# Fused linear attention and squared-ReLU MLP: the second product in f16 from chunk 3, f16 projections from pair 7, denominators summed on GpSimd, Strassen from chunk 13, two matmuls of constants first

## The chip, the cores and the metric

The kernel runs on one core of a Trainium2 chip. A core has five engines that run side by side: PE (TensorE, matrix products), DVE (VectorE), ACT (ScalarE), POOL (GpSimd) and SP (SyncE, which here issues all transfers between the device's memory and the core's own). Each works through its own list of instructions in order and waits on semaphores for the others. The metric is the device time of one execution in microseconds, as a median over runs; lower is better.

## The reference

Two stages. The attention has 8 batches and 8 heads of 576 tokens with 64 dimensions; the features are 128 projections, made positive by two exponentials. The MLP takes the 4608 tokens by 512 dimensions through 2048 hidden units.

```python
def phi(x):
    proj = np.einsum('bhsd,df->bhsf', x, w_phi)
    proj = proj - np.max(np.abs(proj), axis=-1, keepdims=True)
    return np.concatenate([np.exp(proj), np.exp(-proj)], axis=-1)
q_p, k_p = (phi(q), phi(k))
kv = np.einsum('bhsf,bhsd->bhfd', k_p, v)
z = np.sum(k_p, axis=2)
num = np.einsum('bhsf,bhfd->bhsd', q_p, kv)
den = np.einsum('bhsf,bhf->bhs', q_p, z)[..., None] + 1e-06
x = (num / den)            # as 4608 tokens x 512
h = x @ w_in
g = np.maximum(h, 0.0) ** 2
out = g @ w_out
```

All inputs and the output are float32.

## The kernel before

**Attention by pairs.** Two heads of a batch make a pair; there are 32. The first six (`early`, line 779) go a way of their own while the weights are prepared. From pair 6 on, `visit(i)` (973) puts into one stretch of PE the key projections of pair i+1 (`k_main`, `k_tail`), the product of keys and values of pair i (`kv_main`) and the numerators of pair i-1 (line 989). `late(p)` (1036) projects the queries into `pt` (one buffer), finds the largest magnitude of each column with a GpSimd reduction over partitions (1088), subtracts, takes two exponentials into `qe`, and for the denominators weighs them by the key sums into `pt` again (1100, 1102). A transpose and a sum on DVE (1106, 1107), two transfers through device memory, a short DVE tail (1117 to 1120) and further transfers give 1/den as rows in `rb`. `tokens` (934) multiplies by the numerators, scales, and writes x as an f16 pair (high part and remainder) into `ring`.

Before pair 12 (`HALF`) the projections are float32 products. From pair 12 on `narrow` (655) finds the size of k and q (ACT, then a small GpSimd reduction), and splits each into an f16 high part and remainder; the projection is then three f16 products.

**MLP by chunks.** A chunk is 256 tokens (18 of them), a block is 256 hidden units of it (8 a chunk, 144 in all); `moe(c, f)` at 1138 makes one block. The first product, `gemm1` (1164), is 24 f16 matmuls of 256 columns: high by high, high by low, low by high. ACT and DVE form g = relu(h)^2 as `gh` in f32r (float32 bits that PE reads in one pass) and the remainder `gl` in bf16. The second product, `gemm2` (1195), is 12 matmuls of 512 columns: four in f32r against `wh`, eight in bf16 against `wl` and a bf16 copy of w_out. From chunk 14 (`C0`) on, `split_block` (1408) does the second product by Strassen's scheme in f16 instead: seven products of 128 x 256 in three parts, 21 matmuls of 256 columns (1440), with sums and differences on DVE before and after. Of the last chunk the last two blocks (`ENDS`) keep the plain way. Strassen needs bounds: `split_norms` (1253) takes column norms of w_in and row maxima of w_out, `tail_scale` (1289) the norms of a chunk of x, and from them a power of two for the chunk, so that g fits f16.

**The order.** Every step is added to a `Plan` (83) with the engine, an assumed duration, what it comes after and a rank. A planner in the program runs through these with its own clock per engine and writes each engine's list in that order. The ranks of nearly all steps come from a table of characters (`RANKS`) that was fixed beforehand; some steps can go to either of two engines (`other`), and the planner chooses. On the chip nothing is reordered: an engine that waits holds up all behind it.

Of the kernel before, what the change touches and what calls it, by code (L numbers as in the profile page):

```python
# [26 lines left out]
F = 128  # L27
# [7 lines left out]
T = 256  # L35
NCH = NT // T
C0 = 14
ENDS = 2
HALF = 12
LASTB = C0 * T // S  # L40
LOOK = (B - 1 - LASTB) * NP
RING = 6 * T
# [7 lines left out]
LEAD = 44  # L50
# [8 lines left out]
COLD = 1.1  # L59
# [23 lines left out]
class Plan:  # L83
# [73 lines left out]
    def order(self):  # L157
# [13 lines left out]
        mode, moved = WHOLE, 0.0  # L171
# [22 lines left out]
        while done < len(self.ops):  # L194
# [28 lines left out]
            op.start, op.end = t, t + us * (COLD if e == "PE" and t < 125.0 else 1.0)  # L223
# [61 lines left out]
def dve_us(n):  # L285
    return (n + 151) / 960

# [5 lines left out]
def par_us(n):  # L293
    return 0.45 + n * 0.0030
# [7 lines left out]
def tile_kernel(ctx, tc, qp, kp, vp, w_phi, w_in, w_out, out):  # L302
# [100 lines left out]

    pool_start = P.add("POOL", 10.8, lambda: None, [], [], -100.0)
# [166 lines left out]
    def batch_scale(b, rank):  # L571
# [63 lines left out]
    def narrow_weights(rank):  # L635
# [4 lines left out]
            wk[1], wk[0], channels=128, reduce_op=bass_isa.ReduceOp.max), [o, pool_next], [], rank, lock=0.0)  # L640
# [14 lines left out]
    def narrow(p, rank):  # L655
# [10 lines left out]
        o = P.add("POOL", par_us(2), bound, last + [pool_next], uses[:2], rank + 0.1, lock=0.0)  # L666
# [9 lines left out]
        for i, (tag, (raw, ld)) in enumerate(raws.items()):  # L676
# [257 lines left out]
    def tokens(p, nums, rank):  # L934
# [11 lines left out]
        for c0, c1 in cuts:  # L946
# [11 lines left out]
            def low(to=to, c0=c0, c1=c1):  # L958
# [4 lines left out]
                "DVE", dve_us(c1 - c0), lambda to=to, c0=c0, c1=c1: V.tensor_scalar(  # L963
# [72 lines left out]
    def late(p):  # L1036
# [48 lines left out]
        for h in range(2):  # L1085
# [4 lines left out]
                [pt[0], pt[1 + h], pool_next], [("pt", p), ("mx", n)], R(RQ + 0.2), lock=0.0)  # L1090
# [10 lines left out]
                out=y(), in_=qe(0), func=AF.Copy, scale=zc_[p][:, 2 * h:2 * h + 1]), [zc, o], use, R(RQ + 0.8))  # L1101
            o = P.add("DVE", dve_us(S), lambda h=h, qe=qe, y=y: V.scalar_tensor_tensor(  # L1102
# [3 lines left out]
            o = P.add("DVE", dve_us(S), lambda n=n, y=y: V.transpose(yt_["y", n - 2 * EARLY], y()), [o], [("pt", p), ("yt", ("y", n - 2 * EARLY))], R(RQ + 0.9))  # L1106
            dens.append(P.add("DVE", dve_us(S), lambda n=n, h=h: V.tensor_reduce(
                out=d4_[p][:, h, :], in_=yt_["y", n - 2 * EARLY].rearrange("p (b x) -> p b x", x=32), op=ALU.add, axis=AX.X),
                [o], [("yt", ("y", n - 2 * EARLY)), ("d4", p)], R(RQ + 1.0)))

        o = P.add("SP", 0.4, lambda: SP.dma_start(dd_[p], flat(d4_[p])), dens, [("d4", p), ("dd", p)], R(RQ + 1.1),
                  land=1.9, xfer=0.1)
        o = P.add("SP", 0.4, lambda: SP.dma_start(da_[p], dd_[p].rearrange("(a x) y -> x a y", a=4)), [o],
                  [("dd", p), ("da", p)], R(RQ + 1.1), land=1.9, xfer=0.1)

        def inverse():
            V.tensor_reduce(out=dr_[p][:, 0:36], in_=da_[p].rearrange("p a x -> p x a"), op=ALU.add, axis=AX.X)
            V.tensor_scalar(out=dr_[p][:, 0:36], in0=dr_[p][:, 0:36], scalar1=1e-6, scalar2=None, op0=ALU.add)
            V.reciprocal(out=dq[:, :, 0:18], in_=dr_[p].rearrange("p (h x) -> p h x", h=2))
            V.transpose(dt_[p], flat(dq))  # L1120

        use = [("da", p), ("dr", p), ("dt", p)]
        o = P.add("DVE", 0.95, inverse, [o], use, R(RQ + 1.1), lock=4.0)

        def keep():
            for h in range(2):
                SP.dma_start(rd_[p].rearrange("(h x) y -> h (x y)", h=2)[h].rearrange("(b x) -> b x", x=32),
                             dt_[p][0:18, 32 * h:32 * h + 32])

        o = P.add("SP", 0.7, keep, [o], [("dt", p), ("rd", p)], R(RQ + 1.1), land=1.9, xfer=0.1)  # L1130
        spread(p, o, lambda h: rd_[p].rearrange("(h c r) x -> h c (r x)", c=2, h=2)[h].unsqueeze(0).to_broadcast([64, 2, SH]),
               R(RQ + 1.1))


# [3 lines left out]
    def moe(c, f, w_done):  # L1138
# [15 lines left out]
        if f == 0 and split:  # L1154
            tail_scale(c, after)
# [497 lines left out]
```

## Time and profile before

| | us |
|---|---|
| median of 3 runs | 1032.64 (1032.29 to 1034.31) |
| the profiled execution | 1029.46 |
| its span, first to last instruction | 1027.7 |
| busy PE / DVE / ACT / POOL | 994.9 / 824.1 / 740.5 / 169.1 |

The profile is of one execution on its one core. Its page and the answers of its trace are read as follows. A line of the windows has the stretch, then the busy time of each engine in it. A line of the groups has the program line, engine, operation, written and read tiles, shapes, count, busy time and the mean ns of one, then the idle time of the engine ahead of it and what ended it. A line of the timeline or of the chain of waits has the start in us, the duration, and the instructions merged in it. Matmuls are pipelined: one lasts longer from start to end than the distance to the next start, so the cost of one is read from starts.

### The profile page before, as it was taken

How to read it: one execution, taken by the hardware profiler on the slowest of the kernel's cores; microseconds unless marked ns; L12 is line 12 of the kernel's file. 1: busy time of each engine (PE TensorE's matmuls, PEld its weight loads, DVE VectorE, ACT ScalarE, POOL GpSimd, SP SyncE). 2: the span in 40 equal slices, each digit the busy share in tenths (PEclk: the TensorE clock that was granted, in tenths of full speed). 3: DMA queues.
4: the chain of work that ended last, by engine and by line, in shares of the span. 5: the costliest groups of instructions: out<-in, count | busy, mean ns of one | idle time of the engine just before them, and what ended most of it. 6: DMA issues, size and time to landing. Idle time of an engine off the chain costs nothing. (4 is left out here: it accounts for less than half of the span.)

```text
span 1027.7 us, 21125 instructions
## 1 busy us (share of the span) xinstructions
PE 994.9 (97%) x8247; PEld 717.0 (70%) x8310; DVE 824.1 (80%) x1547; ACT 740.5 (72%) x1346; POOL 169.1 (16%) x100
## 2 busy tenths in 40 slices
PE   7879899999999999999999999999999999999998
PEld 5546666676766667667766667667667667888886
DVE  7999887867778885987989889798877889974463
ACT  7999876667678857768877878977667677664462
POOL 0122131031211102202111034311021110000000
PEclk9999999999999999999999999999999999999999
DMA  9744323222222321232323412222111110000000
GB/s 359 262 163 131 135 60 88 66 72 57 63 71 66 82 75 38 62 77 54 105 61 93 97 48 60 69 63 73 41 46 46 25 40 33 1 22 1 22 22 21
DMA packets 92936, 76.28 MB, mean 74 GB/s; under 512 B 61476, under 2 KB 70308, under 8 KB 90788
## 3 DMA queue, kind: packets, MB, share of 16 engines
q1 hardware_dynamic: 92836, 74.93, 25.1%
q8 instruction: 65, 1.06, 0.4%
q14 instruction: 35, 0.29, 0.1%
HBM read 61.18 MB, written 13.68 MB: 73 GB/s over the span
## 5 line engine op out<-in xcount | busy, mean ns | idle before, releaser
L1164 PE MATMUL ph<-ring,win 128*128 128x256 f16 x3456 | 391.8, 273 | 1.4 <-DVE gl L315 1.4
L1164 PEld LDWEIGHTS <-win 128*128 128x128 f16 x3456 | 336.0, 98 | 58.5 <-issue 9.8
L1088 POOL PARTITION_ALL_REDUCE mx<-pt x52 | 116.0, 2232 | 497.7 <-ACT pt L320 196.9
L1195 PE MATMUL po<-wh,gh 128*128 128x512 f32 x456 | 146.0, 441 | 0.0
L1195 PE MATMUL po<-wl,gl 128*128 128x512 bf16 x455 | 118.2, 382 | 0.1
L1176 ACT ACTIVATE r<-ph,cw 128x512 f32<-128x512 f32 x114 | 77.6, 681 | 55.5 <-PE ph L1164 55.1
L1195 PE MATMUL po<-wl,gh 128*128 128x512 bf16 x394 | 107.0, 379 | 5.9 <-issue 3.5
L315 DVE TENSOR_TENSOR gl<-ph,gh 128x512 bf16<-128x512 f32 x114 | 77.3, 678 | 34.9 <-ACT ph L1180 31.3
L1195 PEld LDWEIGHTS po<-wh,gh 128*128 128x128 f32 x456 | 86.1, 189 | 26.2
L1195 PEld LDWEIGHTS <-gh 128*128 128x128 bf16 x456 | 42.0, 98 | 49.1 <-issue 8.2
L1195 PEld LDWEIGHTS <-gl 128*128 128x128 bf16 x456 | 35.3, 98 | 58.3 <-issue 26.7
L1178 ACT ACTIVATE gh<-r 128x512 fp32r<-128x512 f32 x114 | 71.1, 624 | 3.7 <-PE po L1195 1.5
L1180 ACT ACTIVATE ph<-r 128x512 f32<-128x512 f32 x114 | 67.0, 588 | 0.4
L768 PE MATMUL pv<-e,v 128*64 128x256 f32 x512 | 62.8, 389 | 3.2 <-ACT kz L322 2.0
L315 DVE TENSOR_TENSOR qe<-pt,mx 128x576 f32<-128x576 f32 x52 | 39.0, 751 | 20.2 <-POOL mx L1088 18.7
L315 DVE TENSOR_TENSOR v<-qe,gh 128x896 f16<-128x896 f32 x30 | 32.6, 1089 | 27.2 <-ACT gh L1428 27.0
L1093 ACT ACTIVATE qe<-qe 128x576 f32<-128x576 f32 x52 | 35.2, 677 | 20.1 <-DVE qe L315 19.8
L1102 DVE SCALAR_TENSOR_TENSOR pt<-qe,zc,pt 128x576 f32<-128x576 f32 x52 | 42.1, 809 | 9.5 <-ACT pt L1100 9.2
L768 PEld LDWEIGHTS pv<-e,v 128*64 128x64 f32 x512 | 35.0, 141 | 20.7 <-ACT kz L322 2.9
L1413 ACT ACTIVATE r<-ph,cwr 128x512 f32<-128x512 f32 x30 | 20.6, 686 | 34.2 <-PE ph L1164 34.0
L1440 PEld LDWEIGHTS <-gh 128*128 128x128 f16 x420 | 41.1, 98 | 4.8
L1249 POOL PARTITION_ALL_REDUCE n<-n x12 | 22.2, 1848 | 119.3 <-DVE n L1247 79.7
(362 smaller groups left out, 1851.8 us busy)
## 6 DMA issues: line engine op xcount, KB each, us to landing
v<-in_vp_dram SPq DMA_DIRECT2D x32, 320.0 KB
k<-in_kp_dram SPq DMA_DIRECT2D x32, 288.0 KB
q<-in_qp_dram SPq DMA_DIRECT2D x32, 288.0 KB
rb<-rd SPq DMA_DIRECT2D x64, 144.0 KB
out_dram<-o SPq DMA_DIRECT2D x28, 256.0 KB
td<-kvs SPq DMA_DIRECT2D x26, 128.0 KB
kz<-td SPq DMA_DIRECT2D x104, 32.0 KB
zq<-zd SPq DMA_DIRECT2D x104, 2.0 KB
```

The source lines that it names most:

```text
L315: eng.tensor_tensor(out=out_, in0=a, in1=b_, op=ALU.subtract)
L768: PE.matmul(out=to[64 * h:64 * h + 64, 0:256], lhsT=v_[p][:, t, h, :], rhs=e_[2 * p + h][:, t].rearrange("p s f -> p (s f)"), start=t == 0 ...
L1088: o = P.add("POOL", par_us(S), lambda n=n, h=h: G.partition_all_reduce(mx_[n], pt_[p][:, h, :], channels=128, reduce_op=bass_isa.ReduceOp. ...
L1093: o = P.add("ACT", act_us(S), lambda qe=qe: A.activation(out=qe(1), in_=qe(0), func=AF.Exp, scale=-1.0), [o], [("qe", n)], R(RQ + 0.4))
L1102: o = P.add("DVE", dve_us(S), lambda h=h, qe=qe, y=y: V.scalar_tensor_tensor(out=y(), in0=qe(1), scalar=zc_[p][:, 2 * h + 1:2 * h + 2], in ...
L1164: PE.matmul(out=ph[:, j, :], lhsT=win[w][:, t, 128 * ff:128 * ff + 128], rhs=ring[half][x][:, t, c0:c0 + T], start=k == 0, stop=k == 3 * K ...
L1176: o = P.add("ACT", act_us(512, 1), lambda: A.activation(out=r_[n], in_=ph_[bank], func=AF.Relu, scale=cw[:, f, 0:1]), [g1], [("ph", bank), ...
L1178: sq = P.add("ACT", act_us(512), lambda: A.activation(out=gh_[n], in_=r_[n], func=AF.Square), [o], [("r", n), ("gh", n)], Q)
L1180: o = P.add("ACT", 0.59, lambda: A.activation(out=ph_[bank], in_=r_[n], func=AF.Square), [o], [("ph", bank), ("r", n)], Q, other=("DVE", 0 ...
L1195: PE.matmul(out=po_[po[i][1]], lhsT=g[:, j, 128 * i:128 * i + 128], rhs=w[:, j, :], start=(f == (NFP - ENDS if last else 0) and (s, j) == ...
L1249: o = P.add("POOL", par_us(T), lambda: G.partition_all_reduce(n2_[i], n1_[i], channels=128, reduce_op=bass_isa.ReduceOp.add), [o, pool_nex ...
L1440: PE.matmul(out=to, lhsT=l()[:, a], rhs=r(slice(b_, b_ + 1))[:, 0], start=(f == 0 and k == 0 and place % 2 == 0), stop=(f == NFP - 1 - END ...
```

## The change

The table of ranks is replaced, and with it the order of all engines' lists. The planner's assumptions change too: the largest ones are that PE is slow after the start and after a pause (`COLD`, `WARM`, `GAP`, `AGAIN`), that DVE is faster at one form of operation (`pair_us`), and that a GpSimd reduction over partitions and a DVE operation no longer exclude one another (`lock=None`). `LEAD`, a shift of the MLP's ranks, goes from 44 to 52.

- Two float32 matmuls of a constant tile, 480 columns each, stand first on PE.
- `HALF` 12 to 7: pairs 7 to 11 are narrowed and projected in f16.
- Denominators: the DVE transpose and sum, the tail and the transfers between are replaced by a GpSimd sum over partitions, one transfer per head, and the add and reciprocal that the early pairs use.
- From chunk 3 (`CS`) on, `gh` and `gl` are f16 and `gemm2` is three f16 parts. `narrow_out` rescales w_out to an f16 pair in place, after chunk 2. `chunk_scale` takes the place of `tail_scale` for all these chunks, and the first Relu of a block comes after it. `split_norms` is due before chunk 3.
- `C0` 14 to 13: chunk 13 goes by Strassen; `split_out` reads the f16 pair.

```diff
-C0 = 14
+C0 = 13
-HALF = 12
+CS = 3
+HALF = 7
-LEAD = 44
+LEAD = 52
...
+    def warm():
+        for i in range(2):
+            PE.matmul(out=po_[0][:, 0:480], lhsT=ones[:, 0:1].to_broadcast([128, 128]),
+                      rhs=ones[:, 0:1].to_broadcast([128, 480]), start=True, stop=True)
+
+    P.add("PE", 2.3, warm, [], [("po", 0)], -100.0)
...
-            o = P.add("DVE", dve_us(S), lambda n=n, y=y: V.transpose(yt_["y", n - 2 * EARLY], y()), [o], [("pt", p), ("yt", ("y", n - 2 * EARLY))], R(RQ + 0.9))
-            dens.append(P.add("DVE", dve_us(S), lambda n=n, h=h: V.tensor_reduce(
-                out=d4_[p][:, h, :], in_=yt_["y", n - 2 * EARLY].rearrange("p (b x) -> p b x", x=32), op=ALU.add, axis=AX.X),
...
-        o = P.add("DVE", 0.95, inverse, [o], use, R(RQ + 1.1), lock=4.0)
...
+            key = [("yt", ("y", n))]
+            o = P.add("POOL", 3.56, lambda n=n, y=y: G.partition_all_reduce(
+                yt_["y", n], y(), channels=128, reduce_op=bass_isa.ReduceOp.add), [o], [("pt", p)] + key,
+                R(RQ + 0.9), lock=None)
+            dens.append(P.add("SP", 0.5, lambda n=n, h=h: SP.dma_start(
+                den_[p][64 * h:64 * h + 64], yt_["y", n][0:1].rearrange("j (r x) -> j r x", x=9)), [o],
+                [("den", p)] + key, R(RQ + 1.0), land=2.1, xfer=0.1))
+
+        denominators(p, dens, lambda h: rd_[p].rearrange("(h c r) x -> h c (r x)", c=2, h=2)[h].unsqueeze(0).to_broadcast(
+            [64, 2, SH]), R(RQ + 1.1))
...
+        if f == 0 and c == CS:
+            for x in range(NFP):
+                narrow_out(x)
+        if f == 0 and c >= CS:
+            chunk_scale(c, after)
...
+        word = c >= CS
+        by = lambda: cw_[c][:, f:f + 1] if word else cw[:, f, 0:1]
+        gh = lambda: gh_.at(n, [128, 2, T], F16) if word else gh_[n]
+        gl = lambda: gl_.at(gi, [128, 2, T], F16) if word else gl_[gi]
+        use, wait = ([("cwr", c)], [norm_x[c]]) if word else ([], [])
...
+            if word:
+                lo, hi = wout[f][1].bitcast(F16), wout[f][2].bitcast(F16)
+                parts = (gh(), hi), (gh(), lo), (gl(), hi)
+            else:
+                low, near = wout[f][1:]
+                parts = (gh(), highs[f]), (upper(gh()), low), (gl(), near)
...
+        for i in range(2):
+            sums.append(P.add("ACT", act_us(512) + 0.19, lambda i=i: A.activation(
+                out=sx_["nx", 2 * c + i].bitcast(BF16)[:, 0:512].rearrange("p (k t) -> p k t", k=KT),
+                in_=ring[half][0][:, :, c0 + 128 * i:c0 + 128 * i + 128], func=AF.Square, accum_out=nx_[c][:, i:i + 1]),
+                after, [("sx", ("nx", 2 * c + i)), ("nx", c)], rank))
+        o = P.add("POOL", par_us(2), lambda: G.partition_all_reduce(
+            nx_[c][:, 4:6], nx_[c][:, 0:2], channels=128, reduce_op=bass_isa.ReduceOp.add), sums + [pool_next], [("nx", c)], rank, lock=None)
...
+    def narrow_out(f):
+        rank = LEAD + CS * NFP - 4.0 + f
+        places = lambda: (highs[f].bitcast(F32), wout[f][1], wout[f][2].bitcast(F16), wout[f][1].bitcast(F16))
...
+        def hi():
+            A.activation(out=places()[2], in_=places()[0], func=AF.Copy, scale=wts[:, 3:4])
+
+        def rest_of():
+            V.scalar_tensor_tensor(out=d(), in0=places()[0], scalar=wts[:, 3:4], in1=places()[2], op0=ALU.mult, op1=ALU.subtract)
+
+        def lo():
+            V.scalar_tensor_tensor(out=places()[3], in0=places()[1], scalar=wts[:, 3:4], in1=d(), op0=ALU.mult, op1=ALU.add)
+
+        o = P.add("ACT", act_us(1024, 1), hi, [g2_of[(CS - 1) * NFP + f], split_at["w"]], [], rank)
+        o = P.add("DVE", dve_us(1024), rest_of, [o], use, rank, lock=4.0)
+        narrow_w[f] = P.add("DVE", dve_us(1024), lo, [o], use, rank, lock=4.0)
...
-    split_norms(PER_PAIR * 24.0 + 3.0)
+    split_norms(LEAD + (CS - 2) * NFP)
```

More of the change, by code (lines that the diff above doesn't have):

```diff
@@ L58 @@
 RA, RQ, RZ = 1.3, 0.4, 0.3
-COLD = 1.1
+COLD = 1.8
+WARM = 5.0
+GAP = 2.6
+AGAIN = 5.5
 def word(x):
@@ L222, in order @@
             us, _, lock = op.ways[e]
-            op.start, op.end = t, t + us * (COLD if e == "PE" and t < 125.0 else 1.0)
+            if e == "PE" and t > max(cold, free["PE"] + GAP):
+                cold = t + AGAIN
+            op.start, op.end = t, t + us * (COLD if e == "PE" and t < cold else 1.0)
             if lock is not None:
@@ L664, in bound @@
             G.partition_all_reduce(x[:, 0:2], ka_[p], channels=128, reduce_op=bass_isa.ReduceOp.max)
-        o = P.add("POOL", par_us(2), bound, last + [pool_next], uses[:2], rank + 0.1, lock=0.0)
+        o = P.add("POOL", par_us(2), bound, last + [pool_next], uses[:2], rank + 0.1, lock=None)
         def bits():
@@ L1100, in late @@
             o = P.add("ACT", act_us(S, 1), lambda h=h, qe=qe, y=y: A.activation(
-                out=y(), in_=qe(0), func=AF.Copy, scale=zc_[p][:, 2 * h:2 * h + 1]), [zc, o], use, R(RQ + 0.8))
-            o = P.add("DVE", dve_us(S), lambda h=h, qe=qe, y=y: V.scalar_tensor_tensor(
+                out=y(), in_=qe(0), func=AF.Copy, scale=zc_[p][:, 2 * h:2 * h + 1]), [zc, o], use, R(RQ + 0.8), other=(
+                    "DVE", pair_us(S), lambda h=h, qe=qe, y=y: V.tensor_scalar(
+                        out=y(), in0=qe(0), scalar1=zc_[p][:, 2 * h:2 * h + 1], scalar2=None, op0=ALU.mult), 4.0))
@@ L1111, in late @@
[L1111 to L1120, printed above, removed]
@@ L1175, in moe @@
             return
+        word = c >= CS
[3 more added lines that the diff above has]
+        use, wait = ([("cwr", c)], [norm_x[c]]) if word else ([], [])
         o = P.add("ACT", act_us(512, 1), lambda: A.activation(
-            out=r_[n], in_=ph_[bank], func=AF.Relu, scale=cw[:, f, 0:1]), [g1], [("ph", bank), ("r", n)], Q)
-        sq = P.add("ACT", act_us(512), lambda: A.activation(out=gh_[n], in_=r_[n], func=AF.Square),
+            out=r_[n], in_=ph_[bank], func=AF.Relu, scale=by()), [g1] + wait, [("ph", bank), ("r", n)] + use, Q)
+        sq = P.add("ACT", act_us(512), lambda: A.activation(out=gh(), in_=r_[n], func=AF.Square),
                    [o], [("r", n), ("gh", n)], Q)
@@ L1211, in scaled @@
         def scaled():
+            if c >= CS:
+                V.tensor_scalar(out=o_[tt], in0=po_[po[1]], scalar1=ks_[c][:, i:i + 1], scalar2=None, op0=ALU.mult)
+                return
             k = cc[:, tt:tt + 1]
@@ L1215, in store @@
         if c < NCH - 1:
[L1216 removed]
+            o = P.add("DVE", dve_us(DM) + 0.11, scaled, [g2], [po, ("o", tt)] + ([("ks", c)] if c >= CS else []), Q)
             P.add("SP", 0.38, lambda: SP.dma_start(out[128 * tt:128 * tt + 128, :], o_[tt]), [o], [("o", tt)], Q,
@@ L1231, in tile_kernel @@
     wn = sm.tile([128, NFP], F32, name="wn")
-    cc2 = sm.tile([128, 1], F32, name="cc2")
-    last_cc = cc[:, 2 * NCH - 1:2 * NCH]
-    square_of = P.add("DVE", 0.2, lambda: V.tensor_tensor(out=cc2, in0=last_cc, in1=last_cc, op=ALU.mult), [], [], 250.0, lock=4.0)
     wnm = sm.tile([128, 2], F32, name="wnm")
@@ L1349, in split_out @@
             o = P.add("ACT", out_us(256 * n) + 0.09, lambda x=x, src=src: A.activation(
-                out=hi(x), in_=src(), func=AF.Copy, scale=wts[:, 3:4]), [o, split_at["w"]], key + us_ + keep, rank + 0.2)
+                out=hi(x), in_=src(), func=AF.Copy), [o], key + us_ + keep, rank + 0.2)
             o.after += home
-            o = P.add("DVE", dve_us(256 * n), lambda x=x, src=src: V.scalar_tensor_tensor(
-                out=lo(x), in0=src(), scalar=wts[:, 3:4], in1=hi(x), op0=ALU.mult, op1=ALU.subtract),
+            o = P.add("DVE", dve_us(256 * n), lambda x=x, src=src: sub(V, lo(x), src(), hi(x)),
                 [o], key + us_ + keep, rank + 0.3, lock=4.0)
@@ L1374, in sw_home @@
             return cut(*of[:4]), cut(*of[4:]), keep, []
-        g = f // 2
-        home = f"{'lh'[f % 2]}{g}"
-        wait = [("after", x) for x in (2 * g, 2 * g + 1)]
+        home = ("h0", "h1", "h2", "x1", "l0", "l1")[f]
+        wait = [("after", x) for x in (2 * f - 8, 2 * f - 7)] if f > 3 else []
         box = []
```

212 lines of the change are left out of this document (101 added, 111 removed).

## The prediction

> **What bounds the kernel now.** I read the windows first, by stage, because a share over the whole span mixes a start that waits for data with a long stretch that does not.
>
> ```profile
> 0.00:125.00 125.00, 103.19 (x1068) 71.43 (x1071) 108.27 (x173) 108.61 (x189) 17.55 (x12) 0.97 0.58 208
> 125.00:300.00 175.00, 173.18 (x1292) 118.80 (x1305) 140.54 (x277) 119.57 (x226) 32.91 (x17) 1.00 0.27 71
> 300.00:875.00 575.00, 569.80 (x4556) 395.57 (x4601) 486.12 (x924) 433.77 (x798) 115.01 (x69) 1.00 0.24 62
> 875.00:1028.00 153.00, 148.76 (x1338) 131.18 (x1336) 89.19 (x176) 78.50 (x137) 3.59 (x2) 1.00 0.04 15
> ```
>
> The columns are the stretch, its length, then the busy time of PE, PE's weight loads, DVE, ACT and POOL, the granted clock, the DMA share and GB/s. From 125 to 875 us PE is busy 743.0 of 750, so PE's own work sets the end there, and DVE and ACT have room. From 875 on PE is idle 4.2 us, nearly all of it the last result's way out. Before 125 us PE is idle 21.8 us: there the weights and the first pairs are prepared, and DVE and ACT (108 us each) share the bound with the loads. So an edit is worth what it takes out of PE's stream, plus what it changes in the 21.8 us at the start, plus any new stall: PE runs a list fixed in advance and waits in order.
>
> **PE's work.** The chain of waits and the PE timeline give the slots, from one start to the next.
>
> ```profile
> 684.97 2.67 PE po L1195 x12
> ...
> 892.04 1.31 PE pp L1440 x12
> 894.33 1.31 PE pp L1440 x12
> ...
> 923.15 13.10 PE ph L1164 x120
> ```
>
> ```profile
> 1020.08 1.04 PE L1195 MATMUL po<-wl,gl 128*128 128x512 bf16 x4
> 1020.96 0.59 PE L1195 MATMUL po<-wl,gh 128*128 128x512 bf16 x2
> ```
>
> ```profile
> 1020.74 0.38 PE L1195 MATMUL po<-wl,gl 128*128 128x512 bf16 x1
> ```
>
> A second product of one block is 12 matmuls of 512 columns in 2.67 us: 8 in bf16, 4 in f32r. The pace of 16-bit matmuls has three readings. The first product's f16 ones of 256 columns go at 13.10/120 = 0.109 us, hence 0.218 for 512. Four bf16 from 1020.08 to the next start at 1020.96 are 0.22 each. Two take 0.59 where one takes 0.38 from start to end, a step of 0.21. I take 0.216, among the three: twelve f16 make 2.59, so the f32r form costs 0.08 a block over it. The count: chunks 3 to 12 have 80 blocks, with the last chunk's two whole blocks 82, so **6.5 us** go. The ends are 0.03 a block (at 0.22: 2.5 us) and 0.15 (at 0.21: 12 us). This is the largest term and still small, since f32r already runs at nearly this pace; what goes is a few hundredths on 4 matmuls in 12.
>
> Chunk 13 changes to Strassen: 21 matmuls of 256 columns, whose blocks stand 894.33 - 892.04 = 2.29 apart, for 12 in 2.67. Eight blocks by 0.38 are **3.0 us**.
>
> ```profile
> 132.79 0.76 PE L1069 MATMUL pp<-q,wraw 64*128 64x288 f32 x4
> ...
> 133.96 1.04 PE L1195 MATMUL po<-wl,gh 128*128 128x512 bf16 x3
> ...
> 143.22 1.16 PE L703 MATMUL pp<-wraw,k 64*128 64x128 f32 x16
> 144.31 0.44 PE L715 MATMUL pn<-wraw,k 128*64 128x128 f32 x4
> 144.58 1.90 PE L768 MATMUL pv<-e,v 128*64 128x256 f32 x16
> ```
>
> ```profile
> 321.07 0.30 PE L1065 MATMUL pp<-q,whigh 64*128 64x288 f16 x2
> ...
> 321.91 0.50 PE L1164 MATMUL ph<-ring,win 128*128 128x256 f16 x3
> ```
>
> ```profile
> 687.57 0.23 PE L698 MATMUL pp<-whigh,k 64*128 64x128 f16 x2
> ...
> 688.53 1.68 PE L768 MATMUL pv<-e,v 128*64 128x256 f32 x14
> ```
>
> Pairs 7 to 11 go from f32 to f16 projections: q from 1.17 (132.79 to 133.96) to 0.84 (321.07 to 321.91), k from 1.36 (143.22 to 144.58) to 0.96 (687.57 to 688.53). Five pairs by 0.73 are **3.6 us**. Together PE loses 13.1 us.
>
> **The start.** Two matmuls of constants run while PE waits for the first k.
>
> ```profile
> 4.35 2.08 PE L703 MATMUL po<-wraw,k 64*128 64x128 f32 x16 [4.35 <-DMA k<-in_kp_dram]
> ...
> 11.79 2.95 PE L768 MATMUL pv<-e,v 128*64 128x256 f32 x16
> ...
> 22.76 1.95 PE L768 MATMUL pv<-e,v 128*64 128x256 f32 x16 [2.02 <-ACT kz L322]
> ...
> 32.52 1.16 PE L703 MATMUL po<-wraw,k 64*128 64x128 f32 x16
> ```
>
> The same groups take 2.08 at 4.35 us and 1.16 later, 2.95 at 11.79 and 1.95 later, so PE is about half as fast for its first 10 us. If the constants, inside the 4.35 us of waiting, end that, the groups to 15 us lose some 4 us. But 2 us of PE waiting for ACT at 22.76 follow, so part of it only lengthens waits. Between 0 and 4 I take 1.5, the start being bound by loads and by ACT and DVE as much as by PE.
>
> **DVE, ACT and POOL.** The groups by line:
>
> ```profile
> L1106 DVE STREAM_TRANSPOSE yt<-pt 128x576 f32<-128x576 f32 x52 | 40.0, 770 | 0.4
> ...
> L1107 DVE TENSOR_REDUCE d<-yt 128x18 f32<-128x576 f32 x52 | 38.5, 741 | 0.4
> ...
> L1247 DVE TENSOR_REDUCE n<-j 128x256 f32<-128x1024 bf16 x12 | 23.3, 1943 | 2.0 <-POOL n L1249 2.0
> ...
> L1249 POOL PARTITION_ALL_REDUCE n<-n x12 | 22.2, 1848 | 119.3 <-DVE n L1247 79.7 <-DVE xs L1296 24.0 <-DVE wn L1260 15.6
> ...
> L659 ACT ACTIVATE sx<-k 128x576 bf16<-128x576 f32 x20 | 13.6, 678 | 6.4 <-DMA k<-in_kp_dram 6.3
> ...
> L1117 DVE TENSOR_REDUCE dr<-da 32x36 f32<-32x144 f32 x26 | 10.0, 386 | 9.3 <-DMA da<-dd 9.3
> ...
> L1324 DVE TENSOR_TENSOR e<-wh,wl 128x1024 f32<-128x1024 f32 x8 | 9.5, 1210 | 0.0
> ...
> L664 POOL PARTITION_ALL_REDUCE kb<-ka x20 | 8.5, 425 | 18.1 <-ACT sx L659 15.5 <-DVE gl L315 2.5
> L670 DVE TENSOR_SCALAR kb<-kb 128x2 f32<-128x2 f32 x20 | 8.5, 423 | 5.8 <-POOL kb L664 5.6
> L1271 ACT ACTIVATE j<-wh 128x1024 bf16<-128x1024 f32 x8 | 8.4, 1050 | 1.8 <-DVE n L1247 1.8
> ```
>
> The denominators take off DVE 52 transposes and 52 sums, 78.5 us, and 26 short tails that begin with L1117 (10.0 us); the add and the reciprocal that replace the tails are of its kind. SP issues five transfers a pair for six. GpSimd gets 52 sums of 576 columns, which no run here has; its sums took 1.85 us for 256 columns, its small reduction 0.43 for 2, so by a straight line 0.43 + 574 x 0.0056 = 3.6 us, 189 us in all over some 700. GpSimd has the time (169 us busy now). For PE all this is worth nothing directly: DVE already had room.
>
> What comes in early is the load I weigh more. The norms of w_in and the row sums of w_out move from the middle to before chunk 3: 16 ACT passes of 1.05, 8 DVE sums of 1.94. The new rescaling of w_out costs 8 more ACT passes and 16 DVE passes of 1.21. Pairs 7 to 11 need two ACT sizes and two ACT roundings, about 0.75 each (an estimate from L659), and two DVE differences like it. That is 25 + 15 = 40 us of ACT and 16 + 19 + 8 = 43 of DVE, less some 20 of denominators, mostly into 125 to 300 us, where ACT and DVE have 260 of 350 busy: after it 323, 92%. I cost it at nothing, as PE has only 1.8 us idle there and chunks 0 to 2 stand ready as work; without that cover it is the second rival. The scale per chunk adds a wait ahead of each chunk's first Relu: two ACT passes, a short GpSimd reduction and a DVE chain; behind that Relu stand ACT's queue and then the second product. The ring's columns are written blocks ahead, and the first product (2.6 us) runs beside, so nothing again; if all 15 chunks waited 0.5 us, 7 us.
>
> **GpSimd against DVE.** Two rows of the timelines:
>
> ```profile
> 515.31 1.26 DVE L670 TENSOR_SCALAR kb<-kb 128x2 f32<-128x2 f32 x1 [0.73 <-POOL kb L664]
> ```
>
> ```profile
> 515.17 2.21 POOL L1088 PARTITION_ALL_REDUCE mx<-pt  x1
> ```
>
> A DVE instruction on two columns takes 1.26 us because a GpSimd reduction began 0.14 before it; it is let go at 516.57, 0.8 us before that reduction ends. So a reduction holds DVE for at most its first 1.4 us or so, when DVE has work of the kind it blocks; 52 more could hold it 73 us at the very most, of the 88 that are freed. The Trainium skill (SBUF — State Buffer, "SBUF: two separate sides") says that the pair of ports that these engines share is locked for the whole instruction and that the loser blocks fully. The trace agrees that one blocks, not that it lasts the whole instruction. By that rule the sums would hold DVE up to 52 x 3.6 = 187 us, and the result would be that of the first rival.
>
> **The sum.** From the profiled execution's 1029.46 us: less 6.5, 3.0, 3.6 and 1.5, nothing for the rest: 14.6, hence 1014.9. The median of the runs shown, 1032.64, lies 3.2 above that execution; I add it and predict **1018**. The terms' own ends (PE 9 to 19, start 0 to 4, chunk waits 0 to 7) make 1010 to 1031.
>
> **Rivals.** First, slower: the sums sit in the loop that holds the one projection buffer pt.
>
> ```profile
> 653.08 0.30 PE L1065 MATMUL pp<-q,whigh 64*128 64x288 f16 x2
> ```
>
> ```profile
> 675.56 0.77 DVE L1106 STREAM_TRANSPOSE yt<-pt 128x576 f32<-128x576 f32 x1
> ```
>
> ```profile
> 678.39 0.29 PE L1065 MATMUL pp<-q,whigh 64*128 64x288 f16 x2
> ```
>
> Pair 25 takes pt at 653.08 and gives it back at 676.33, 23.3 us later; the next takes it 25.3 us after the first. A sum of 3.6 for a transpose of 0.77 adds 2.8, a second sum behind the first up to 1.4, two locked DVE steps up to 2.8: up to 30, over the period. From the point at which the hold passes 25.3 us PE's next projection, and with its fixed order all behind it, is late. An average of 1.3 us over 25 pairs is 33 us: 1051. Against it: that hold has waits in it that a new order can take out, and one buffer's slack is all that it needs. 8%.
>
> Second, the early load starves PE between 125 and 300 us. At the start's rate (21.8 idle of 125) it would be 30 us; a third of it takes 10 us back: 1028. For it speaks the 92%, against it that PE then has other work ready. 15%.
>
> Third, f16 is no faster than f32r in this stream, or the chunks' waits eat it, and only chunk 13, the projections and the start remain, 8.1: 1024.5. 7%.
>
> Fourth, better: the start loses all 4 us of slow clock and some 6 of its 21.8 idle, as DVE is freed: 1009.5. 12%.
>
> **How the numbers follow.** The forecast has 58%. The range 1006 to 1031 takes in the terms' ends and the second to fourth rivals; it leaves out the first and the outer part of the second. A change below 0.2%, 2 us, cannot be told from none here. Faster needs under 1030.6: the forecast, the third, the fourth and most of the second, 88%; the second's rest gives 3% for the same; 9% slower, mainly the first.
>
> **What would show it.** Second products of 2.59 a block; L1440 with 8 blocks more; PE busy near 980; groups at 4 to 15 us as fast as later ones; GpSimd sums near 3.6 with DVE instructions beside them stretched by about 1 us; PE still over 98% busy from 125 to 300. It is wrong if PE waits for pt's copies or for the chunk's Relu, or if second products stay at 2.67.

## The result and the profile after

| | before | after |
|---|---|---|
| median | 1032.64 (1032.14 to 1035.8, 6 runs) | 1097.54 (1094.33 to 1103.06, 6 runs) |
| the profiled execution | 1029.46 | 1094.33 |
| its span | 1027.7 | 1092.5 |

The ratio is 1.0629, 95% interval 1.0608 to 1.0651: 65 us slower, where 15 us faster was forecast. The page of after gives the busy time and, in its chain of waits, what the end hangs on:

```profile
PE 1010.3 (92%) x8441; PEld 702.9 (64%) x8454; DVE 858.4 (79%) x1555; ACT 775.9 (71%) x1440; POOL 383.9 (35%) x168
...
PE 46%; DVE 29%; ACT 11%; DMA 6%; issue 4%; POOL 2%; SPq 1%; DVEq 0%; ACTq 0%; POOLq 0%
```

78.5 us of transposes and sums were to leave DVE and 43 us of early load to come in, yet its busy time did not fall by some 35 us: it rose from 824.1 to 858.4, and 29% of the chain that ended last runs through it. The windows of after, columns as before:

```profile
0.00:125.00 125.00, 94.95 (x953) 61.57 (x955) 96.29 (x160) 100.03 (x177) 15.21 (x12) 0.89 0.58 204
125.00:300.00 175.00, 159.89 (x1236) 109.03 (x1246) 161.28 (x270) 142.32 (x256) 82.89 (x39) 0.96 0.22 58
300.00:875.00 575.00, 547.11 (x4416) 352.25 (x4415) 470.13 (x858) 417.80 (x798) 266.06 (x115) 0.99 0.25 65
```

PE is idle 30.1 us in the first stage (21.8 before), 15.1 in the second (1.8) and 27.9 in the third (5.2). The second product became cheaper, as forecast. In the timeline of after one block's second product in f16 starts 2.59 us after the other's (2.67 before):

```profile
707.43 1.89 PE L1204 MATMUL po<-wl,gh 128*128 128x512 f16 x8
709.15 1.03 PE L1204 MATMUL po<-wl,gl 128*128 128x512 f16 x4
710.02 1.89 PE L1204 MATMUL po<-wl,gh 128*128 128x512 f16 x8
```

So PE waits, and the view of waits names DVE for most of it (between 125 and 875 us; columns: who waits for whom, us in total, times, longest):

```profile
PE ph L1161 <- DVE gl L327: 11.9, 6, 3.1
PE pp L1076 <- DVE e L742: 8.2, 3, 5.3
PE pn L1076 <- DVE pw L435: 6.2, 2, 4.1
PE pp L709 <- DVE k L695: 5.3, 4, 2.4
```

**A wait costs twice.** Behind some of its longer waits PE is also slow. In the timeline of after a first product, 24 matmuls, takes 4.97 us behind a wait of 4.12; at 217 us, with no wait before it, one takes 2.78:

```profile
185.00 0.39 PE L1076 MATMUL pn<-q,whigh 64*128 64x288 f16 x1 [4.12 <-DVE pw L435]
185.84 4.97 PE L1161 MATMUL ph<-ring,win 128*128 128x256 f16 x24
```

Between 184 and 190 us the granted clock was 0.50. The view of this line, of before and then of after (shortest, median and longest in ns, then the first and the last start in us), shows that no such matmul was slow before:

```profile
L1164 PE MATMUL ph<-ring,win x3456: 269/273/283, 90.4 to 1013.6; 128*128 128x256 f16 x192
```

```profile
L1161 PE MATMUL ph<-ring,win x3456: 269/273/421, 110.7 to 1081.0; 128*128 128x256 f16 x192
```

**Why DVE got longer.** The groups, first of before and then of after:

```profile
L315 DVE TENSOR_TENSOR qe<-pt,mx 128x576 f32<-128x576 f32 x52 | 39.0, 751 | 20.2 <-POOL mx L1088 18.7 <-PE pv L989 1.5
L750 DVE TENSOR_TENSOR ez<-e 128x512 f32<-128x512 f32 x52 | 35.9, 690 | 6.0 <-ACT e L736 5.6
```

```profile
L1120 POOL PARTITION_ALL_REDUCE yt<-pt x52 | 200.2, 3850 | 156.0 <-DVE pt L1115 101.4
...
L327 DVE TENSOR_TENSOR qe<-pt,mx 128x576 f32<-128x576 f32 x52 | 47.1, 907 | 8.6 <-POOL mx L1099 6.6
...
L761 DVE TENSOR_TENSOR ez<-e 128x512 f32<-128x512 f32 x52 | 41.2, 792 | 11.4 <-ACT e L747 11.0
```

The sums take 3.85 us on average, near the estimate of 3.6, and the shortest 3.59. But the subtraction `qe` rose to 907 ns from 751, and `ez` to 792 from 690, with nothing changed in either. The views of one line, first of before and then of after (shortest, median and longest in ns), show that most of them last as ever and a few very long:

```profile
L684 DVE SCALAR_TENSOR_TENSOR k<-k,kb,k x20: 773/806/819, 274.7 to 786.4; 128x576 f16<-128x576 f32 x20
```

```profile
L695 DVE SCALAR_TENSOR_TENSOR k<-k,kb,k x25: 797/818/3116, 163.6 to 822.0; 128x576 f16<-128x576 f32 x25
```

The longest one, in the timeline of after:

```profile
378.16 3.60 POOL L1120 PARTITION_ALL_REDUCE yt<-pt  x1 [2.42 <-DVE pt L1115]
378.19 3.12 DVE L695 SCALAR_TENSOR_TENSOR k<-k,kb,k 128x576 f16<-128x576 f32 x1
```

It starts 0.03 us behind a sum and lasts 3.12 instead of 0.80; less its own 0.80 it was let go 2.35 us after the sum's start, 1.25 before that ends. I took every DVE instruction that overlaps one of the 52 sums and lasted over 0.15 us longer than its like: there are 42, together some 70.8 us longer. In the ten that were let go soonest it was 2.34 us after the sum's start. All 42 read from the core's memory alone: 35 read two arrays there, seven are a `TENSOR_SCALAR`, which reads one (as `kb<-kb`, the row from which the prediction read the hold). Instructions that read PE's result banks were not touched: 23 of the 106 `gl` overlap a sum, and the longest of all takes 695 ns.

```profile
L327 DVE TENSOR_TENSOR gl<-ph,gh x106: 630/681/695, 117.6 to 1083.2; 128x512 f16<-128x512 f32 x82, 128x512 bf16<-128x512 f32 x24
```

It works the other way too: 23 of the sums last 0.1 to 1.7 us longer than 3.59, and in each of these DVE was at work, when the sum began or within 0.1 us of it, on such an instruction. That is where the average of 3.85 comes from.

**The start.** A second loss has nothing to do with sums. The chain, the ACT timeline and the PE timeline of after show it:

```profile
28.58 9.38 DMA den<-sx
```

```profile
38.06 0.74 ACT L586 ACTIVATE sx<-v 128x640 bf16<-128x640 f32 x1 [10.52 <-DMA den<-sx]
```

```profile
40.40 2.19 PE L896 MATMUL pv<-qe,kz 128*64 128x288 f32 x8 [11.65 <-ACT kvs L334]
```

The small transfer of an early pair's denominators (4.5 KB) leaves from `sx`, a scratch tile that others share. It lands only after 9.4 us, as weight loads of 1 MB are under way. In the new order ACT's very next instruction rewrites `sx`, so ACT stands 10.5 us, and DVE and PE behind it. Before, the same transfer left at 30.4 us, and the next write of `sx` came at 39.5, when fourteen other ACT instructions had run:

```profile
30.42 0.71 SPq L910 DMA_DIRECT2D den<-sx  x1
```

```profile
39.52 0.72 ACT L575 ACTIVATE sx<-v 128x640 bf16<-128x640 f32 x1
```

The first product of block 0 starts at 110.7 us instead of 90.4.

### The profile page after: what moved, and what is told of

It is laid out like the page before. It is cut to its first block, busy times and chain, and to the rows that moved or that the text cites. A ratio compares the mean times of both kernels' runs of the same rounds, so it can differ in the third digit from the quotient of the medians.

```text
span 1092.5 us, 21663 instructions
## 1 busy us (share of the span) xinstructions
PE 1010.3 (92%) x8441; PEld 702.9 (64%) x8454; DVE 858.4 (79%) x1555; ACT 775.9 (71%) x1440; POOL 383.9 (35%) x168
## 4 chain that ended last, share of the span: by engine, by line
PE 46%; DVE 29%; ACT 11%; DMA 6%; issue 4%; POOL 2%; SPq 1%; DVEq 0%; ACTq 0%; POOLq 0%
PE ph L1161 18%; PE po L1204 9%; PE pv L779 3%; PE pp L1477 2%; PE po L1477 2%; DVE k L695 2%; DVE qe L327 2%; DVE ring L970 2%; PE pn L1477 2%; DVE pt L1115 2%; DVE gl L327 2%; DMA raw4i<-in_w_in_dram 2%; DVE sw L327 2%; PE pn L1000 1%; PE pv L1477 1%
## 5 line engine op out<-in xcount | busy, mean ns | idle before, releaser
L1120 POOL PARTITION_ALL_REDUCE yt<-pt x52 | 200.2, 3850 | 156.0 <-DVE pt L1115 101.4
L1204 PE MATMUL po<-wl,gh 128*128 128x512 f16 (+1 forms) x740 | 179.4, 381 | 3.5 <-ACT e L747 1.8
L1204 PEld LDWEIGHTS <-gh 128*128 128x128 f16 (+1 forms) x752 | 71.8, 98 | 84.6 <-issue 10.0
L1204 PE MATMUL po<-wl,gl 128*128 128x512 f16 (+1 forms) x423 | 109.9, 382 | 0.0
L327 DVE TENSOR_TENSOR gl<-ph,gh 128x512 f16<-128x512 f32 (+1 forms) x106 | 72.1, 681 | 26.2 <-ACT ph L1182 20.4
L1204 PEld LDWEIGHTS <-gl 128*128 128x128 f16 (+1 forms) x424 | 39.7, 98 | 51.6 <-issue 5.8
L1178 ACT ACTIVATE r<-ph,cwr 128x512 f32<-128x512 f32 x82 | 55.5, 677 | 24.0 <-PE ph L1161 23.7
L1180 ACT ACTIVATE gh<-r 128x512 f16<-128x512 f32 (+1 forms) x106 | 66.1, 623 | 2.9 <-PE po L1204 2.0
L1465 ACT ACTIVATE gh<-qe 128x896 f16<-128x896 f32 x38 | 36.0, 947 | 31.8 <-PE pv L1477 13.8
L1459 DVE TENSOR_TENSOR qe<-qe 128x256 f32<-128x256 f32 (+1 forms) x114 | 36.4, 374 | 27.6 <-ACT qe L1455 27.4
L1450 ACT ACTIVATE r<-ph,cwr 128x512 f32<-128x512 f32 x38 | 26.0, 684 | 39.1 <-PE ph L1161 39.0
L761 DVE TENSOR_TENSOR ez<-e 128x512 f32<-128x512 f32 x52 | 41.2, 792 | 11.4 <-ACT e L747 11.0
```

What stands on the lines that cost most here:

```text
L327: eng.tensor_tensor(out=out_, in0=a, in1=b_, op=ALU.subtract)
L761: o = P.add("DVE", dve_us(512), lambda n=n: V.tensor_tensor(out=ez_[n].rearrange("p t x -> p (t x)"), in0=e_[n][:, 0:2].rearrange("p t s f ...
L1120: o = P.add("POOL", 3.56, lambda n=n, y=y: G.partition_all_reduce(yt_["y", n], y(), channels=128, reduce_op=bass_isa.ReduceOp.add), [o], [ ...
L1178: o = P.add("ACT", act_us(512, 1), lambda: A.activation(out=r_[n], in_=ph_[bank], func=AF.Relu, scale=by()), [g1] + wait, [("ph", bank), ( ...
L1180: sq = P.add("ACT", act_us(512), lambda: A.activation(out=gh(), in_=r_[n], func=AF.Square), [o], [("r", n), ("gh", n)], Q)
L1204: PE.matmul(out=po_[po[i][1]], lhsT=g[:, j, 128 * i:128 * i + 128], rhs=w[:, j, :], start=(f == (NFP - ENDS if last else 0) and (s, j) == ...
```

## The experiments

Theory: the sums hold DVE while they use a port that both share (call it the port), and `sx` costs the start. Rivals: the sums are late results in the loop that holds `pt` (the latency); the new early load; an order that suits the chip badly whatever it holds. "Single run" marks a time that was measured once; six runs of after lie between 1094.33 and 1103.06, so differences of a few us between such times mean little.

### No sums (e1), and sums that nobody reads (e2)

In e1 the GpSimd instruction is left out:

```diff
-            o = P.add("POOL", 3.56, lambda n=n, y=y: G.partition_all_reduce(
-                yt_["y", n], y(), channels=128, reduce_op=bass_isa.ReduceOp.add), [o], [("pt", p)] + key,
+            o = P.add("POOL", 3.56, lambda: None, [o], [("pt", p)] + key,
```

In e1 and e2 the transfer takes a row of `pt` in place of the sums, and 1e15 is added to what it brings:

```diff
-                den_[p][64 * h:64 * h + 64], yt_["y", n][0:1].rearrange("j (r x) -> j r x", x=9)), [o],
+                den_[p][64 * h:64 * h + 64], pt_[p][0:1, h, :].rearrange("j (r x) -> j r x", x=9)), [o],
```

> The changed kernel in its own order, without its 52 GpSimd sums of 576 columns: the denominators are read from one row of what would be summed, and 1e15 is added to them, so the output is left near zero. Theories: (A) the sums hold DVE through the port that the two engines share, and PE's fixed order waits behind DVE: 1040 us, with DVE busy some 70 us less than the 858 of the changed kernel. (B) it is the time that a sum takes in the chain of a pair (3.6 us and more, pt held for it), not the port: also near 1040, but DVE busy about the same. (C) the sums do not matter, and the new order, the narrowing and the moved norms cost the time: over 1080.

> The changed kernel in its own order; the 52 GpSimd sums run, but the denominators are read from the summed tile's source, so that no one waits for a sum's result; only the next pair's use of pt does. 1e15 is added to the denominators, so the output is left near zero. (A) port: over 1080 us, DVE instructions beside a sum still stretched by up to 2.3 us. (B) the sum's time in the chain: 1040 to 1060. (C) as the changed kernel, about 1097.

Measured, a single run each: e1 1045.28, e2 1100.30, the kernel before beside them 1031.69. Both have the order of after. The page of e1:

```profile
PE 996.1 (95%) x8441; PEld 698.2 (67%) x8454; DVE 785.5 (75%) x1555; ACT 774.4 (74%) x1440; POOL 185.1 (18%) x116
```

With the same 1555 instructions DVE is busy 72.9 us less than in after, about the 70.8 of stretch, and 38.6 less than before, near the 35 that the prediction's own terms make. In e2 the sums run and no result of theirs is used, and nothing is gained: the stretch is 78.9 us. It is that the sums run, not that they come late. Of the 49 us between the spans of after and e1, 14.2 are busy time of PE (1010.3 for 996.1) with the same 8441 matmuls: PE is slow behind waits (74 of the first product's matmuls last over 350 ns in after, 19 in e1). The hold of `pt`, too, can be read in after itself, in the view of waits (us in total, times, longest):

```profile
ACT pt L332 <- POOL yt L1120: 2.4, 2, 1.8
```

The copies wait 2.4 us in all for sums to give `pt` back. Nor do sums keep DVE waiting for the maxima queued behind them on GpSimd: in the same view DVE waits 21.9 us for these (`kb` and `qe`), and 22.9 in e1.

### Sums added to the kernel before (e5)

```diff
-... lambda n=n, y=y: V.transpose(yt_["y", n - 2 * EARLY], y()), [o], ...
+... lambda n=n, y=y: (V.transpose(yt_["y", n - 2 * EARLY], y()), G.partition_all_reduce(
+    y(), y(), channels=128, reduce_op=bass_isa.ReduceOp.add)), [o], ...
```

> The kernel before, in its own order, with 52 GpSimd sums of 576 columns added, in place on what the DVE transposes have just read; no result of them is used. (A) port: 1060 to 1090 us, DVE busy 60 to 80 us more than 824. (B) time in the chain: 1033 to 1045, since only the reuse of pt waits for a sum. (C) 1033 to 1036.

Measured: 1092.10, a single run, 60 above the kernel before and 2 above (A). The stretch is 58.6 us, in 41 DVE instructions. PE's waits for DVE in this run, and the waits of the copies into `pt`:

```profile
PE ph L1164 <- DVE gl L315: 22.1, 15, 3.4
```

```profile
ACT pt L320 <- POOL pt L1106: 13.0, 7, 4.7
ACT pt L322 <- POOL pt L1106: 7.8, 3, 4.3
```

None of the other edits is in it. The sums alone, in the old order, cost nearly what the whole change cost. But here the copies wait 20.8 us for sums to give `pt` back, which they did not before, so part of the 60 can be that hold; how much is not shown. PE is busy 1010.5 us with the same 8247 matmuls that took 994.9 before.

### The denominators' transfer from a tile of its own (e3)

```diff
-        first, second = copy(SH, lambda: sx_["d", p][:, 0:SH], lambda: pn_["d", p][:, 0:SH])
+        first, second = copy(SH, lambda: yt_["d", p][:, 0:SH], lambda: pn_["d", p][:, 0:SH])
...
-            den_[p], sx_["d", p][0:128:32, 0:SH].rearrange("j (r x) -> j r x", x=9)), [o], use + [("den", p)],
+            den_[p], yt_["d", p][0:128:32, 0:SH].rearrange("j (r x) -> j r x", x=9)), [o], use + [("den", p)],
```

> The changed kernel in its own order, but the early pairs' denominators go out from tile yt, not from sx, so that ACT's next write to sx need not wait for that transfer behind 1 MB loads of weights. (A) the wait of 10.5 us at 28 us is what the start lost most of its 20 us to: 1083 to 1087 us, chunk 0 begins near 98 us. (B) the start is bound by the landing of the weights or by the amount of ACT and DVE work anyway: 1094 to 1099, chunk 0 near 108.

Measured: 1083.74, a single run, 13.8 below after. The windows show the gap gone; first after, then e3:

```profile
25.00:50.00 25.00, 10.66 (x123) 7.55 (x119) 12.37 (x19) 12.04 (x18) 0.00 (x0) 0.80 0.59 228
```

```profile
25.00:50.00 25.00, 20.93 (x270) 14.64 (x266) 24.18 (x43) 23.63 (x42) 0.00 (x0) 1.00 0.75 276
```

PE, DVE and ACT do twice the work in the same 25 us.

### Both at once (e9)

The edits of e1 and e3 together.

> The run without the GpSimd sums (1045 us; denominators from one row, 1e15 added) with the early pairs' denominators going out from tile yt as well. If the sums and that wait are all that the change loses: 1033 us or less, down to 1018 if the whole 20 us of the start return. If the start has another cause: 1043 to 1046.

Measured: 1031.51, a single run. 13.8 for the tile and 52.3 for the sums add up: 1097.5 - 66.1 = 1031.4 (that it fits to 0.1 is luck with single runs). So the two losses are separate, and without them the change is worth nothing, where PE's terms alone were to bring 13. One place where that goes is seen in e9's windows:

```profile
125.00:300.00 175.00, 164.00 (x1318) 111.19 (x1328) 163.12 (x286) 145.59 (x265) 53.66 (x32) 0.99 0.23 60
```

PE is idle 11.0 us between 125 and 300, 9.2 more than before, with DVE and ACT at 309 of 350. The largest wait there is for `e`, with no sums in the run:

```profile
PE pp L1076 <- DVE e L742: 5.9, 2, 5.3
```

### The assumption in the planner (e4)

```diff
-... reduce_op=bass_isa.ReduceOp.max), [o, pool_next], [], rank, lock=None)
+... reduce_op=bass_isa.ReduceOp.max), [o, pool_next], [], rank, lock=0.0)
```

and six more like it: in the planner a GpSimd reduction and a DVE operation exclude one another again.

> The changed kernel with one assumption of its planner set back: a GpSimd reduction over partitions and DVE operations exclude one another (seven places). Nothing is computed differently; only the order changes, and the planner now knows of the conflict. (A) port: 1050 to 1080 us, since DVE's other work can stand beside the sums, with DVE busy nearer to 800. (B) and (C): within 10 us of 1097, since the sums' time and the other work stay.

Measured: 1173.38, a single run, where 1050 to 1080 was expected. The sums still stretch DVE by 62.2 us. The ranks come from a table made under the other assumption, and with this one they give another and far worse order. The run says nothing of the price of the sums.

### Denominators on DVE, in the order of after (e6, e7)

e6 puts the DVE transpose, sum and tail of before back into after and keeps its table of ranks; e7 adds the edit of e3.

```diff
-            o = P.add("POOL", 3.56, lambda n=n, y=y: G.partition_all_reduce(
-                yt_["y", n], y(), channels=128, reduce_op=bass_isa.ReduceOp.add), [o], [("pt", p)] + key,
...
+            o = P.add("DVE", dve_us(S), lambda n=n, y=y: V.transpose(yt_["y", n - 2 * EARLY], y()), [o], [("pt", p), ("yt", ("y", n - 2 * EARLY))], R(RQ + 0.9))
+            dens.append(P.add("DVE", dve_us(S), lambda n=n, h=h: V.tensor_reduce(
+                out=d4_[p][:, h, :], in_=yt_["y", n - 2 * EARLY].rearrange("p (b x) -> p b x", x=32), op=ALU.add, axis=AX.X),
...
+        o = P.add("DVE", 0.95, inverse, [o], use, R(RQ + 1.1), lock=4.0)
```

> The changed kernel with the denominators of the kernel before (two DVE transposes and sums a pair, tail, transfers), planned with the same table of ranks. (A) port: as without the sums, 1040 to 1055 us, though DVE gets its 88 us back. (C) DVE's work matters as much as its locks: over 1070.

> The same with the early pairs' denominators going out from tile yt: both suspected losses are taken away and all gains on PE are kept. 1025 to 1040 us if both causes hold, 1018 if nothing else is lost; 1040 to 1055 if the start has another cause.

Measured: e6 1092.01 (ratio 1.0589, 1.0529 to 1.065), e7 1078.33 (1.044, 1.0415 to 1.0465). The own tile is worth 13.7 again; that e6 would come near 1050, and e7 to 1055 at most, was wrong. Two things are mixed here, the 88 us of DVE work that are back and an order that was not made for them.

### The same in orders of their own (e11, e12)

For both the ranks were sought anew, for the steps of each and with the holds that these runs showed. e11 is e7 in such an order. e12 puts the early load off as well, and with it gives up the f16 projections of pairs 7 to 11 and two chunks of the f16 second product:

```diff
-CS = 3
-HALF = 7
+CS = 5
+HALF = 12
```

> The changed kernel with the denominators of before (DVE transpose and sum), the early denominators sent from a tile of their own, and an order of all engines' lists that was made anew for just these steps, with a GpSimd reduction holding DVE for 1.2 us (maxima), as measured. (A) What was left in the two runs with DVE denominators (1092, 1078) was an order made for other steps: 1028 to 1040, as in the run without sums and with the own tile (1031.5). (B) DVE, with the early load and the denominators both, is itself too full: above 1055.

> The parts of the change that were gains on PE, without the sums on GpSimd and with the early load put off: denominators on DVE as before, second product in f16 from chunk 5 instead of 3, projections in f16 from pair 12 as before, Strassen from chunk 13, constants first, early denominators from a tile of their own, order made anew for these steps. (A) PE loses 66 blocks by 0.08 = 5.3, chunk 13 gives 3.0, the start up to 1.5: 9.8 below 1032.6, so 1023; 1022 to 1029 with some of it lost to the order. (B) The early load still starves PE between 125 and 300 us by the 9 us that the run without sums showed: 1030 to 1036.

Measured: e11 1044.04 (ratio 1.0101, 1.0074 to 1.0129), e12 1034.25 (1.001, 0.9991 to 1.0028). Of the 45 us that e7 lies above before, the order was 34; e11 still lies between (A) and (B). Most of what is left in e11 stands where the early load is; the windows of e11 and of e12:

```profile
125.00:300.00 175.00, 162.58 (x1332) 111.02 (x1332) 169.93 (x321) 145.55 (x266) 51.45 (x32) 1.00 0.25 65
```

```profile
0.00:125.00 125.00, 106.06 (x1054) 71.47 (x1055) 107.98 (x182) 110.51 (x193) 16.97 (x12) 0.92 0.60 217
125.00:300.00 175.00, 172.95 (x1326) 118.02 (x1325) 157.96 (x299) 129.84 (x243) 50.31 (x27) 1.00 0.24 64
```

With DVE at 169.93 of 175 us PE loses 12.4 there; with less load, 2.0, as before. Yet e12 is no faster than before. It missed (A), 1022 to 1029, and (B) has the wrong place, for between 125 and 300 us nothing is lost. Its block 0 comes 4.8 us later than before (95.2 for 90.4), with PE's granted clock at 0.92 in the first 125 us for 0.97. What took the rest of the 8.3 us of matmul time that it saves was not told apart.

### PE's gain alone (e10)

```diff
-g, w = ((gh_[n], highs[f]), (upper(gh_[n]), low), (gl_[gi], near))[s]
+g, w = ((upper(gh_[n]), low), (upper(gh_[n]), low), (gl_[gi], near))[s]
```

The f32r part of the product is left out; 16-bit matmuls stand in its place.

> The kernel before, in its own order, with one edit: in the second product the four f32r matmuls of a block (gh against wh) read the 16-bit words that the second four read (upper half of gh, wl), so that all twelve are 16-bit; that part of the product is left out and replaced by a wrong one. (A) PE's own work is the bound and a 16-bit matmul saves what the slots say, 2.67 to 2.59 a block: chunks 0 to 13 and two blocks of the last have 114 whole blocks, 114 x 0.08 = 9.1 us, all of it seen: 1023 to 1025. (B) A gain on PE is given back, because the steps of DVE and ACT between the products set the pace: above 1030.

Measured: 1027.87 (ratio 0.9938, 0.9915 to 0.9961), 5.5 below before (4.0 to 8.8 by the interval), between (A) and (B). The same stretch in the timelines of before and of e10:

```profile
444.91 1.03 PE L1195 MATMUL po<-wl,gh 128*128 128x512 bf16 x4
...
450.25 1.03 PE L1195 MATMUL po<-wl,gh 128*128 128x512 bf16 x4
```

```profile
444.58 1.89 PE L1195 MATMUL po<-wl,gh 128*128 128x512 bf16 x8
...
449.76 1.89 PE L1195 MATMUL po<-wl,gh 128*128 128x512 bf16 x8
```

Two blocks take 5.18 for 5.34: 0.08 a block, as the slots said. From the first block to the last, the two traces differ by 4.1 us of the 9.1. Followed from block to block up to 855 us, e10 gains 8.2 us and gives back 4.3 in eleven places, by 1.0 at most. The waits point to DVE for it; between 434 and 860 us e10 has these, which before has at 0.3 us or not at all:

```profile
PE pp L1065 <- DVE e L731: 1.3, 1, 1.3
PE po L1195 <- DVE o L1213: 1.1, 2, 0.7
```

### The constants (e13)

To e9, the order of all else kept:

```diff
-    P.add("PE", 2.3, warm, [], [("po", 0)], -100.0)
+    P.add("PE", 2.3, lambda: None, [], [("po", 0)], -100.0)
```

> The kernel without sums and with the own tile (1031.51 in one look, block 0's first product at 97.0 us), less the two matmuls of constants; the order of all else is the same. The denominators of the late pairs are left out as there. (A) The constants shorten the start: the groups between 4 and 15 us take some 4 us more (as in the kernel before: 2.08 and 2.95 for 1.16 and 1.95), block 0's first product comes at 98.5 to 101, the time is 1.5 to 4 us above: 1033 to 1036. (B) The start is set by the loads and by ACT and DVE: block 0 within 1 us of 97.0 and the time within 1 us of 1031.5.

Measured: 1032.51 (ratio 0.9993, 0.9978 to 1.0008); block 0 at 96.4 us, for 97.0 with them. The ratio is to the kernel before; against e9's 1031.51 it is 1.0 us, at the edge of (B), and from a single run of e9. (B): no gain is seen. The timelines of e9 and of e13 show why:

```profile
6.23 1.16 PE L841 MATMUL ph<-wraw,q 64*128 64x128 f32 x16
...
11.76 0.65 PE L779 MATMUL pv<-e,v 128*64 128x256 f32 x2 [1.00 <-ACT e L747]
13.00 3.60 PE L779 MATMUL pv<-e,v 128*64 128x256 f32 x14 [0.59 <-ACT e L747]
```

```profile
6.66 1.98 PE L841 MATMUL ph<-wraw,q 64*128 64x128 f32 x16 [0.33 <-DMA q<-in_qp_dram]
...
12.71 1.94 PE L779 MATMUL pv<-e,v 128*64 128x256 f32 x14 [0.59 <-ACT e L747]
```

With the constants PE is fast at 6 us; but then it waits several times, and at 13 us it is slow where without them it is fast. In after the same group is fast with them (1.94), and still the next group starts no earlier, at 14.80 for 14.59 in e13: the groups ahead wait for ACT. The gain is spent by 15 us.

## Why the prediction was wrong

**The step that failed** is in "DVE, ACT and POOL" and "GpSimd against DVE": "For PE all this is worth nothing directly: DVE already had room", with the hold taken as "at most its first 1.4 us or so" and weighed as "73 us at the very most, of the 88 that are freed". Two errors are in it. The hold was read from a GpSimd maximum and carried over to a sum that lasts longer; a sum holds DVE for 2.34 us, not 1.4 (and in the 1.4 the instruction's own 0.15 was counted: the maxima hold it 1.1 to 1.25). And the time held was set against time freed, as if a DVE microsecond were the same wherever it falls. The freed work had been fitted into gaps; the hold falls on whatever stands next in DVE's fixed list, up to 2.3 us at a time, and often that was a step that PE awaits. The 70.8 us of stretch were about the size of the bound; the sums cost 52 us in after (e1) and 60 in the kernel before (e5, where part can be the hold of `pt`), for a term put at zero. Of the 49 us between the spans of after and e1, 14 are no wait but matmuls that take longer; the prediction weighed a slow PE for the start alone.

**The rule that was weighed.** The Trainium skill (SBUF — State Buffer, "SBUF: two separate sides") says that whichever starts first gets the shared port pair for the whole instruction and that the other fully blocks. The traces disagree with "whole": DVE is let go 2.34 us into a sum of 3.59. They agree that DVE waits in full until then, and that the one that starts first holds up the other: a sum that finds DVE at such work waits too. By that rule the result was to be the first rival's, and in direction it was.

**The first rival** had 8% and 1051. Of its parts the locked DVE steps decided, not the hold of `pt` (2.4 us of waits); and they made PE late for `gl`, `e` and `k`, not for `pt`, so its path was another one. Its price, 33 us, was under the 52 found, and it was given too little chance, for the prediction had the lock in its own rows.

**The start** was to gain 0 to 4 us and lost 14. The prediction counted the instructions of the start and not the shared tiles under a new order: a transfer's source and the next writer of it. The gain itself was not seen (e13): "part of it only lengthens waits" was all of it.

**PE's terms** were right in their slots. A second product takes 2.59. Strassen's blocks in chunk 13 stand 2.29 apart, here two in the chain of waits of after:

```profile
984.02 1.31 PE pp L1477 x12
986.31 1.31 PE pp L1477 x12
```

But that "an edit is worth what it takes out of PE's stream" was too much: of 9.1 us in e10 5.5 came through (4.0 to 8.8), at PE 99% busy. What PE saves brings it sooner to results that are not there yet.

**The second rival**, the early load, was right in place and size: put at 10 us, 9.2 of new idle time in e9, and 10.4 more in e11 than in e12. It could not be seen in the result under the larger losses. The third, f16 no faster, was wrong.

**The marks.** PE was to stay over 98% busy from 125 to 300 us: it was 91%. DVE beside the sums was to be stretched by about 1 us: it was up to 2.3. PE's busy time was to fall to about 980: it is 1010.3, and 996.1 even in e1, for the same matmuls count more where PE is slow (0.89 granted in the first stage of after, 0.97 before). That is not all of it: in e10, where each block takes 0.08 less, busy time fell by 1.3 us only, to 993.6, and why stays open. The scale per chunk was costed at nothing. The view of waits puts one wait of PE down to it, of 2.4 us, but the timeline shows what PE waited for there, a split of `k` that a sum had stretched:

```profile
PE pp L709 <- DVE xs L1313: 2.4, 1, 2.4
```

```profile
717.50 3.08 DVE L695 SCALAR_TENSOR_TENSOR k<-k,kb,k 128x576 f16<-128x576 f32 x1
720.50 0.14 DVE L1313 TENSOR_REDUCE xs<-nx 128x1 f32<-128x2 f32 x1
```

The products of `k` start at 720.6 us, when that split has ended.

So 65 us = 52 (sums) + 14 (tile), and the rest about zero (-1): gains of PE of 13 at most against 9 of early load and what is given back in waits. The last is argued from e9, e10 and e13; no single run shows its parts.

## What to carry to other kernels

Work moved to GpSimd isn't free for DVE: before it is costed, look in the trace for DVE instructions that grow beside GpSimd ones, take the longest of a line against its median, and price a hold by where it falls in the chain, not against DVE's idle time. Ask too whether a wait on PE makes the matmuls behind it slow. When an order is made anew, look for transfers whose source is a shared tile, and who writes it next. At 99% busy a gain on PE is an upper bound; here 4.0 to 8.8 of 9.1 us came through. And where a view puts a wait down to an instruction of 0.14 us, look at the one before it in the timeline.

## What the hardware showed

- A GpSimd sum over partitions of 576 columns takes 3.59 us and holds a DVE instruction that reads two arrays from the core's memory, or a `TENSOR_SCALAR` that reads one array there, for its first 2.34 (four `TENSOR_SCALAR` of one column took 153 ns beside sums); the maxima of 576 columns hold it 1.1 to 1.25. If such an instruction is running, the sum waits for its end, by up to 1.7 us in after. Sums over columns (28 `d<-yt` that start in its first 2.34 us in e5, at most 752 ns for a median of 740) and reads of PE's result banks run beside it undisturbed, and so did two transposes from the core's memory (e5, 711 and 767 ns).
- A transfer of 4.5 KB took 9.4 us to land at the start, while the loads of 1 MB ran.
- PE, once fast, can be slow again after a wait: in after a granted clock of 0.50 from 184 to 190 us follows 4.12 us without work; behind gaps of 1.00 and 0.59 us a group of 14 matmuls took 3.60 instead of 1.94 (e9 at 13 us), and in e12 the group of 16 in this row of its timeline takes 2.17, behind a wait of 2.59, for the 1.16 of others. How long a wait it takes the runs do not fix: in after the first of these groups followed gaps of 0.54 and 0.59 and took 1.94.

```profile
10.44 2.17 PE L721 MATMUL po<-wraw,k 64*128 64x128 f32 x16 [2.59 <-DVE qm L859]
```
